# Loads of four batches moved to the head of slabs, and the tile-mode products of a slab joined into one burst, in a fused attention and feed-forward kernel

## Chip, cores, metric

One NeuronCore of a Trainium2 chip. The metric is the device time of one execution in microseconds (us). All runs used here are fast except one execution of the kernel before (480.15 us, left out of all means). A ratio is the mean time of one kernel's fast runs over that of the other's of the same rounds, so it is not quite the ratio of the medians quoted. Kernels are compared only within the same rounds.

## The reference, cut

```python
# q, k, v: 8 batches x 8 heads x 576 rows x 64, float32
q_s = softmax(q, axis=-1)              # along the 64
k_s = softmax(k, axis=2)               # along the 576 rows
kv  = einsum('bhsd,bhse->bhde', k_s, v)      # 64 x 64 a head
x   = einsum('bhsd,bhde->bhse', q_s, kv)     # back to 576 x 64 a head
# x as 4608 tokens x 512
h = x @ w_in                           # 512 -> 2048
g = h * sigmoid(beta * h)
out = g @ w_out                        # 2048 -> 512
```

The feed-forward part is nearly all of TensorE's work: 1152 wide matmuls, at the 0.2158 us that one takes in slab 7 about 249 of the 271.8 us that TensorE is busy (an estimate from the profile before). The attention part of batch b must be ready before the tokens of batch b enter it.

## The kernel before

The tokens are cut into nine slabs of 512: slab b holds the first 512 rows of batch b, slab 8 the 64 remaining rows of all batches. A slab is *pass 1* (64 matmuls of 128x512 with `w_in`, each group of four drained by a SiLU on ScalarE) and *pass 2* (64 with `w_out`). The attention products of the next batches are slipped between the matmuls of pass 2. They use TensorE as four 64x64 tiles at once, four products to a *quad*: 72 key-value products for a batch (eight heads, nine row groups), 8 output products, and every second slab 16 remainder products.

```python
        def kv_quads(b, bks, halves=(0, 2)):       # 36 products for each half
            i = b % 2
            for a in halves:
                for j in range(NG):                # NG = 9
                    for hp, ro, co in quad(a):
                        p = slice(ro, ro + 64)
                        tile_mm(bks[hp % 2], ro, co, VW * (a // 2), D + 1, EK[i][p, hp, j, :],
                                VB[i][p, hp, j, 0:D + 1], j == 0, j == NG - 1,
                                [("ekc", i, hp), ("vb", i, hp, 0), ("vb", i, hp, 1), ("vone", i)])
            for y in range(2 if 2 in halves else 0):
                ...    # VectorE: reciprocal of the sums, KVC = products x reciprocal

        def block(b):
            if b + 1 < B:
                kv_a(b + 1)                        # first half of the next batch
            out_quads(b, (5, 6, 7, 0))             # 8 output products, 4 copies to XT
            if b % 2 and b > 1:
                outr_quads(b, (1, 2))              # 16 remainder products
        ...
            elif t < 7:                            # slab t: what is slipped in, and after how many matmuls
                todo = [(94, lambda: block(t + 1))]
                if t + 2 < B:
                    todo += [(112, lambda: kv_b(t + 2))]   # second half
        ...
            for b in late:                         # pass 2 of slab t, b = t + 2
                exp_q(b)
                ...
                if b + 2 < B and t > 1:
                    load(b + 2)
```

Slots count a slab's matmuls, so slots 65 to 128 are pass 2. The buffers of K (`EK`) and V (`VB`) are double, one for even and one for odd batches.

Every operation is recorded with what it reads and writes; a write waits for all earlier readers of the same buffer. Semaphores are then planned so:

```python
        for op in self.ops:
            op.deps = [d for d in op.deps if not (d.eng == PE and op.eng == PE and d.slot is None)]
            for d in op.deps:
                d.inc = True                       # d will increment its engine's semaphore
        ...
            elif op.inc:                           # numbered in order, one count an engine
                counts[key] = counts.get(key, 0) + 1
                op.count = (key, counts[key])
        ...                                        # a waiter then waits only for the highest count
```

The softmax here doesn't subtract the row's maximum and nothing guards it: scores larger than these inputs give would overflow.

## Time and profile before

| | before |
|---|---|
| time, median (fast runs) | 283.36 us (283.06 to 283.49, 3 runs) |
| span of the profiled run | 280.5 us |
| TensorE busy, granted clock | 97%, 1.00 |
| slabs 1 to 6, start to start | 16.96*, 29.63, 29.35, 29.22, 29.09, 28.41 us |
| slab 7 (wide matmuls alone) | 27.62 us |

*Slab 1 from the start of its pass 2, since its pass 1 is mixed with slab 0. The lengths are differences of the start times of the first pass 1 matmul of each slab, in the view of TensorE in order of time; worked out before rounding, so the last digit can differ by one from the rounded starts; the prediction shows the starts of slabs 2 to 7, and pass 2 of slab 1 starts at 59.38. TensorE, 97% busy, bounds the kernel, so what a slab takes above 27.62 us is what its small products cost.

### The profile page before, as it was taken

Reading aid. Unit: us, or ns where it says so; the run is one execution under the profiler, and the core shown is the slowest. Engines: PE = TensorE matmul, PEld = TensorE weight load, DVE = VectorE, ACT = ScalarE, POOL = GpSimd, SP = SyncE. Lnnn points to the kernel's source line nnn. Section 1 sums busy time; section 2 is a strip of 40 time slices with the busy share of each in tenths; the row PEclk is TensorE's granted clock in tenths of the full one; section 3 lists DMA queues with packets and bytes.
Section 4 is the critical chain, followed back from the end, with each engine's and each line's share of the span. In section 5 each row is a group of like instructions: output and inputs, shape, how many; then the busy total and the mean of one; then the engine's idle time right before and its main releaser. Section 6 shows DMA issues by size and latency. Waiting matters only on the chain.

```text
span 280.5 us, 4478 instructions
## 1 busy us (share of the span) xinstructions
PE 271.8 (97%) x1836; PEld 132.9 (47%) x1870; DVE 104.6 (37%) x211; ACT 169.0 (60%) x242; POOL 36.7 (13%) x56
## 2 busy tenths in 40 slices
PE   7899999999999999999999999999999999999995
PEld 3545454445445544545454444444444444444443
DVE  4754786217490058003740363035704100110012
ACT  5768687989477735794479537871751176017500
POOL 6630041116104030300050000000000000000000
PEclk9999999999999999999999999999999999999999
DMA  7999999999999999509990034001700020011022
GB/s 246 373 390 402 388 382 305 377 332 249 252 371 214 353 301 408 101 7 306 347 108 4 0 128 98 0 4 64 180 1 0 40 112 0 0 74 78 0 72 78
DMA packets 42044, 50.10 MB, mean 179 GB/s; under 512 B 20900, under 2 KB 29348, under 8 KB 40872
## 3 DMA queue, kind: packets, MB, share of 16 engines
q1 hardware_dynamic: 41072, 48.77, 57.1%
q10 hardware_dynamic: 952, 1.06, 1.1%
q8 instruction: 14, 0.23, 0.3%
q14 instruction: 6, 0.05, 0.1%
HBM read 36.71 MB, written 9.44 MB: 165 GB/s over the span
## 4 chain that ended last, share of the span: by engine, by line
PE 84%; DMA 8%; SPq 3%; DVE 2%; issue 1%
PE PS L390 84%; DMA O2S<-in_moe_w_in_dram 4%; DMA O2S<-in_moe_w_out_dram 4%; SPq L645 1%; SPq L261 1%; DVE QS L356 1%; DVE WOUT L638 1%; SPq L251 0%; PE PS L388 0%; DVE WIN L649 0%; DVE KVC L527 0%; DVE RC L525 0%; DVE QI L357 0%; DVE O2S L799 0%
## 5 line engine op out<-in xcount | busy, mean ns | idle before, releaser
L723 ACT ACTIVATE GT<-PS,BETA 128x512 bf16<-128x512 f32 x144 | 96.8, 689 | 72.9 <-PE PS L390 72.9
L390 PE MATMUL PS<-WOUT,GT 128*128 128x512 bf16 (+2 forms) x571 | 126.4, 373 | 2.2 <-issue 1.4
L390 PE MATMUL PS<-XT,WIN 128*128 128x512 bf16 x564 | 125.8, 379 | 0.6
L390 PEld LDWEIGHTS PS<-XT,WIN 128*128 128x128 bf16 x576 | 60.6, 106 | 63.1 <-ACT GT L723 0.4
L390 PEld LDWEIGHTS PS<-WOUT,GT 128*128 128x128 bf16 x592 | 56.0, 98 | 64.2 <-issue 1.0
L778 DVE COPY O2S<-PS 128x512 f32<-128x512 f32 x33 | 22.6, 685 | 109.6 <-PE PS L390 109.5
L375 POOL CAST VB<-VF 128x576 bf16<-128x576 f32 x29 | 21.5, 741 | 77.9 <-DMA VF<-in_v_dram 43.8
L356 DVE TENSOR_REDUCE QS<-EQ 128x8 f32<-128x512 bf16 (+1 forms) x22 | 20.0, 910 | 14.9 <-ACT EQ L320 14.9
L320 ACT ACTIVATE EQ<-QF 128x512 bf16<-128x512 f32 x32 | 17.8, 616 | 2.4 <-DMA QF<-in_q_dram 2.2
L339 ACT ACTIVATE EK<-KF 128x1152 bf16<-128x1152 f32 (+1 forms) x16 | 15.9, 1035 | 1.8 <-DMA KF<-in_k_dram 1.6
L358 DVE TENSOR_TENSOR EQ<-EQ,QI 128x1024 bf16<-128x1024 bf16 (+1 forms) x14 | 15.8, 1128 | 0.5
L540 DVE CAST XT<-PS 128x512 bf16<-128x512 f32 x12 | 7.7, 685 | 17.3 <-PE PS L390 17.3
L540 ACT CAST XT<-PS 128x512 bf16<-128x512 f32 x12 | 6.4, 589 | 11.2 <-PE PS L390 11.2
L358 POOL TENSOR_TENSOR EQ<-EQ,QI 128x512 bf16<-128x512 bf16 x8 | 8.3, 1042 | 27.4 <-DVE QI L357 27.1
L390 PEld LDWEIGHTS PS<-VB,EK 64*64 64x64 bf16 x504 | 6.5, 107 | 5.9 <-issue 4.9
L390 PE MATMUL PS<-VB,EK 64*64 64x65 bf16 x504 | 8.3, 193 | 0.1
L525 DVE RECIPROCAL RC<-PS 128x2 f32<-128x2 f32 x12 | 2.0, 164 | 13.5 <-PE PS L390 13.5
L390 PE MATMUL PS<-XT 128*128 128x512 f32 x6 | 5.5, 1088 | 1.5 <-DVE XT L221 1.5
L723 ACT ACT_TABLE_LOAD x5 | 6.4, 1283 | 0.1
L332 ACT ACTIVATE EKD<-KF 64x576 bf16<-64x576 f32 (+1 forms) x6 | 5.0, 841 | 1.0 <-DMA KF<-in_k_dram 0.9
L357 DVE RECIPROCAL QI<-QS 128x8 f32<-128x8 f32 (+1 forms) x22 | 5.0, 225 | 0.8
L339 ACT ACT_TABLE_LOAD x4 | 5.1, 1283 | 0.1
(62 smaller groups left out, 86.3 us busy)
## 6 DMA issues: line engine op xcount, KB each, us to landing
out_dram<-O2S SPq DMA_DIRECT2D x8, 1024.0 KB, 5.6
QF<-in_q_dram SPq DMA_DIRECT2D x30, 256.0 KB, 6.3
KF<-in_k_dram SPq DMA_DIRECT2D x6, 1152.0 KB, 8.0
VF<-in_v_dram SPq DMA_DIRECT2D x6, 1152.0 KB, 10.9
KF<-in_k_dram SPq DMA_DIRECT2D x8, 288.0 KB, 8.4
VF<-in_v_dram SPq DMA_DIRECT2D x8, 288.0 KB, 8.7
WST<-in_moe_w_in_dram SPq DMA_DIRECT2D x8, 256.0 KB, 8.0
O2S<-in_moe_w_in_dram SPq DMA_DIRECT2D x4, 512.0 KB, 11.7
```

What stands on the lines that cost most here:

```text
L261: add(engs[c % len(engs)], lambda e, a=a, o=o: e.dma_start(o, a), w=[(name, i, hp) for hp in range(c * n, c * n + n)], slot=f"{name}{i}_{c}")
L320: add(ACTE, lambda e, o=o, a=a: e.activation(o, a, ACT.Exp), r=[("qf", i, hp)] if b < 2 else [("qf", i, hp, x) for x in ((2, 3) if hp % 2 ...
L332: add(ACTE, lambda e: e.activation(o, a, ACT.Exp), r=[("kf", i, h) for h in hps], w=[("ek", i, h, e_) for h in hps])
L339: add(ACTE, lambda e: e.activation(o, a, ACT.Exp), r=[("kf", i, h) for h in range(hp, hp + n)], w=[("ekc", i, h) for h in range(hp, hp + n)])
L356: add(DVE, lambda e: e.tensor_reduce(s_, a, AX.X, ALU.add), r=ks, w=[("qs", i, hp0)])
L357: add(DVE, lambda e: e.reciprocal(v_, s_), r=[("qs", i, hp0)], w=[("qi", i, hp0)])
L358: add(eng, lambda e: e.tensor_tensor(a, a, vb, ALU.mult), r=ks + [("qi", i, hp0)], w=ks)
L375: add(eng, lambda e: (e.copy if eng == ACTE else e.tensor_copy)(o, a), r=[("vf", i, hp), ("vone", i)], w=[("vb", i, hp, h) for h in ((0, 1 ...
L390: add(PE, lambda e: e.matmul(o, l, r_, start=start, stop=stop, tile_position=tp), r=r, w=w, bank=[bk])
L540: add(eng, lambda e, eng=eng, bk=bk, hp=hp: (e.copy if eng == ACTE else e.tensor_copy)(XT[i][:, hp, :], PS[bk][:, :]), r=[("ps", bk)], w=[ ...
L723: add(ACTE, lambda e: e.activation(GT[:, f, :], PS[bk][:, :], ACT.Silu, scale=BETA[:, f:f + 1]), r=[("ps", bk), "beta"], w=[("gt", f)], ba ...
L778: add(eng, lambda e: (e.copy if eng == ACTE else e.tensor_copy)(O2S[t % 2][:, u, :], PS[bk][:, :]), r=[("ps", bk)], w=[("o2", t % 2, u)], ...
```

## The change

Two intents: no loads beside the small products of pass 2, and one entry into tile mode a slab for two. The diff, cut (the functions were only split into products and copies, so that all products of a burst come before all copies):

```diff
         def block(b):
+            rem = b % 2 and b > 1
             if b + 1 < B:
-                kv_a(b + 1)
-            out_quads(b, (5, 6, 7, 0))
-            if b % 2 and b > 1:
-                outr_quads(b, (1, 2))
+                kv_prods(b + 1, (1, 2), (0, 2))
+            out_prods(b, (5, 6, 7, 0))
+            if rem:
+                outr_prods(b, (1, 2))
+            out_evac(b, (5, 6, 7, 0))
+            if rem:
+                outr_evac(b, (1, 2))
+            if b + 1 < B:
+                kv_evac(b + 1, (1, 2))
 ...
-                         (116, lambda: block(2)), (124, lambda: kv_b(3))]
+                         (116, lambda: block(2))]
             elif t < 7:
-                todo = [(94, lambda: block(t + 1))]
-                if t + 2 < B:
-                    todo += [(112, lambda: kv_b(t + 2))]
+                todo = [(104, lambda: block(t + 1))]
 ...
             if 2 <= t < 7:
+                if t < 5:
+                    load(t + 2 if t == 2 else t + 3)
 ...
-                if b + 2 < B and t > 1:
-                    load(b + 2)
 ...
-                    load(4)
```

## The prediction

> **What bounds the kernel now.** I read the page's busy shares first, then the chain that ended last, then TensorE alone in order of time, and last the few microseconds around the tile-mode products in a stage with loads and in one without.

> ```profile
> PE 271.8 (97%) x1836; PEld 132.9 (47%) x1870; DVE 104.6 (37%) x211; ACT 169.0 (60%) x242; POOL 36.7 (13%) x56
> ...
> PEclk9999999999999999999999999999999999999999
> ...
> PE 84%; DMA 8%; SPq 3%; DVE 2%; issue 1%
> ```

> TensorE is busy 97% of the span at its full clock, and 84% of the chain is TensorE; the 8% of DMA and most of the rest lie in the first 38 us, which the change does not touch. So only what shortens TensorE's own stream can help. TensorE in order of time, from slab 4 on (start, us, engine, group):

> ```profile
> 135.32 13.98 PE L390 MATMUL PS<-XT,WIN 128*128 128x512 bf16 x63
> ...
> 164.54 13.98 PE L390 MATMUL PS<-XT,WIN 128*128 128x512 bf16 x63
> ...
> 193.63 13.98 PE L390 MATMUL PS<-XT,WIN 128*128 128x512 bf16 x63
> ...
> 222.05 13.98 PE L390 MATMUL PS<-XT,WIN 128*128 128x512 bf16 x63
> 235.86 13.98 PE L390 MATMUL PS<-WOUT,GT 128*128 128x512 bf16 x63
> 249.67 13.98 PE L390 MATMUL PS<-XT,WIN 128*128 128x512 bf16 x62
> ```

> Slab 7 holds nothing but 128 wide matmuls: 249.67 - 222.05 = 27.62 us, or 0.2158 us each. What any other slab takes above 27.62 is the price of its tile-mode products. Slab 2 starts at 76.34, slab 3 at 105.97, slab 4 at 135.32 (the same view, earlier). Their excesses are: slab 2 2.01, slab 3 1.73, slab 4 1.60, slab 5 1.47, slab 6 0.79. Slabs 2 and 4 have equal work (key-value products of one batch, the output products and the remainder products), and so have slabs 3 and 5 (no remainder). Yet 2 costs 0.41 more than 4, and 3 costs 0.26 more than 5. The timeline shows where, first for slab 2 and then for slab 4:

> ```profile
> 97.09 0.34 PEld L390 LDWEIGHTS PS<-QT,KVC 64*64 64x64 bf16 x8
> 97.37 0.62 PEld L390 LDWEIGHTS PS<-QTR,KVC 64*64 64x64 bf16 x16
> 98.25 3.83 PE L390 MATMUL PS<-WOUT,GT 128*128 128x512 bf16 x17 [0.16 <-issue]
> 102.01 0.44 PEld L390 LDWEIGHTS PS<-VB,EK 64*64 64x64 bf16 x36 [0.42 <-issue]
> 102.73 3.40 PE L390 MATMUL PS<-WOUT,GT 128*128 128x512 bf16 x15 [0.16 <-issue]
> ```

> ```profile
> 155.99 0.15 PEld L390 LDWEIGHTS PS<-QT,KVC 64*64 64x64 bf16 x8
> 156.24 0.39 PEld L390 LDWEIGHTS PS<-QTR,KVC 64*64 64x64 bf16 x16
> 156.90 3.83 PE L390 MATMUL PS<-WOUT,GT 128*128 128x512 bf16 x17 [0.16 <-issue]
> 160.66 0.37 PEld L390 LDWEIGHTS PS<-VB,EK 64*64 64x64 bf16 x36 [0.42 <-issue]
> 161.30 3.40 PE L390 MATMUL PS<-WOUT,GT 128*128 128x512 bf16 x15 [0.16 <-issue]
> ```

> Two things show. Each entry into tile mode stops the weight loads for 0.42 us, and each exit leaves 0.16 us of TensorE idle, though nothing is being waited for. And all small products run slower in slab 2. The sums by stretch give the one difference I can name (the last two columns are the DMA share and GB/s):

> ```profile
> 97.00:103.00 6.00, 5.68 (x105) 3.37 (x94) 2.55 (x5) 2.36 (x3) 1.34 (x3) 1.00 1.14 300
> 126.80:132.50 5.70, 5.38 (x67) 2.70 (x66) 1.89 (x3) 2.36 (x3) 0.00 (x0) 1.00 0.95 306
> 155.50:161.50 6.00, 5.68 (x116) 2.99 (x117) 2.83 (x7) 2.48 (x4) 0.00 (x0) 1.00 0.00 0
> ```

> Loads were running in slabs 2 and 3, and none in slab 4. The granted clock was 1.00 in all three.

> [...] 0.44 against 0.37 us for 36 weight loads. [...] I count this cost, without knowing its mechanism.

> **The change part by part.** No work is added or removed. TensorE's order changes only from slab 1 on.

> *One burst for two.* In slabs 2 to 5 the 36 later key-value products leave slot 112 and the first burst moves from slot 94 to one joint burst at slot 104; in slab 1 slots 116 and 124 become 116. The separate burst's price, without loads: from 156.90 to 161.30 stand 18 wide matmuls (94 to 112), 4.40 - 18 x 0.2158 = 0.52 us. With loads: 98.25 to 102.73, 0.60 us. What 36 such products cost inside a burst: slab 5's first burst is 1.47 - 0.52 = 0.95 (36 key-value and 8 output products); the remainder is (1.60 - 0.52) - 0.95 = 0.13; slab 6's burst has 8 output and 16 remainder products for 0.79, so 8 outputs cost 0.66 and 36 key-value products 0.95 - 0.66 = 0.29. Saved per merge: 0.52 - 0.29 = 0.23 without loads; with loads I take 0.21 (0.60 less an estimated 0.39). All of it is on the path.

> *No loads beside the burst.* Slab 1: batch 4's loads leave it (issued from 69.88, burst at 72.12; batch 3's last remainder load lands at about 72.04), so its burst should run at the quiet rate: 0.26, as between slabs 3 and 5. Slab 3: batch 7's loads (from 124.74) move to slab 4's head, and batch 6's (issued 96.86) to slab 3's head, issued at about 107 to 111 and landed by some 122, before the burst near 127.5: 0.26. Slabs 4 and 5 had no loads beside their bursts already: 0. Slab 2: batch 5's loads still follow batch 4's loads and three transposes on the one SyncE queue, so I expect them issued from about 88 on and in flight until about 103, around the burst at about 98.5. I count 0 there; if it were quiet it would be 0.41.

> The sum: slab 1 0.21 + 0.26, slab 2 0.21, slab 3 0.23 + 0.26, slabs 4 and 5 0.23 each: 1.63 us. Vector and scalar work is the same in number; only its order moves. After the joint burst VectorE has two XT copies (1.29), the remainder copies (0.74) and the key-value pair (about 0.9): 2.9 us, and 24 wide matmuls (5.2 us) remain before pass 1 wants XT and banks 0 to 2. In slab 1 only 12 remain (2.6 us), but pass 1 wants first XT (about 2.0 us after the products) and bank 1 only four matmuls later; it fits.

> **The rivals.** *A late load stalls slab 2.* Batch 4's loads now start behind the store of slab 1, at about 78, and pass 2 of the same slab uses them from 91. The page has K landing a median 8.0 us and V 10.9 us after their issue, so K lands near 89.5 and V near 92.5; ScalarE wants K at 92.35, after its table load; the casts of V take 2.9 us and end near 95.5, the burst is at 98.5. Slack 3 us; a miss would cost 1 to 2 us, 283 to 284. For it: a 1 MB store stands ahead, and loads alone needed 14.4 us from first issue (69.88) to the first cast of V (84.24), with a store in the midst. Against it: even 14.4 us after 78 gives 92.4.

> *Late transposes stall slab 2 or 4.* The transposes of the next batch now stand behind a whole load. In slab 4 that load has eight small remainder pieces and took SyncE 10.4 us to issue before (124.74 to 135.14). From 136 that ends at about 146.5; two transposes and the remainder's take 4 to 5 us more, and land some 3 us later, at about 154; the burst is near 157. Slack about 3 us; again about 1 us if missed, 282.8.

> *The transfers do not slow the products at all* and slabs 4 and 5 were quicker for another reason (place in the program). Then only the merging pays: 1.1 us, 282.4. Against it: the slow and fast rates split exactly by whether the DMA share was near 1 or 0, in four slabs. *Slab 2 quiet too*: 281.4.

> **The range and the chances.** 283.49 - 1.63 = 281.86; the quick runs of before were 283.49 and 283.06, so I say 281.8. The rivals span 281.4 to about 283, with 0.3 us between runs: 281.0 to 282.8. Two per cent is 5.7 us, more than all excesses in slabs 1 to 5 that the change touches could return; a gain that large is out of reach, a loss that large needs stalls in several slabs.

> **What would show it.** Right: slabs 4 and 5 shorter by 0.23 us each (29.0 and 28.86), slab 3 near 28.86 with its weight loads at the 0.15 us rate, one 0.42 us stop per slab, slab 2 near 29.4 and still at the slow rate. Wrong: TensorE idle in front of the burst with a releaser such as the V casts, the K exponentials or a transposed QT, at about 98 or 157 us; a pass 1 that now waits for XT; or a slab 3 burst that is slow although no load runs.

The wide matmuls took the same time with loads and without, 13.81 us from start to start for pass 1 of slab 2, at a DMA share of 1.11, and for that of slab 7, at 0.18. The 0.44 against 0.37 us is the contrast to it: 36 small weight loads in slab 2 and in slab 4.

## The result

The changed kernel is slower by 0.4%, a small loss but clear of the noise: 284.57 us median (284.09 to 285.02, 4 runs) against 283.36; ratio 1.0044, 95% interval 1.0022 to 1.0067. Executions over 1.5% slower than the fastest of the same kernel are left out of the means. The profiled spans are 282.3 against 280.5 us. The forecast of 281.8 (281.0 to 282.8) missed, in sign too.

The same slab lengths, from the same view, say where:

| slab | before | after | difference | predicted |
|---|---|---|---|---|
| 1 (pass 2) | 16.96 | 17.59 | +0.63 | -0.47 |
| 2 | 29.63 | 30.27 | +0.64 | -0.21 |
| 3 | 29.35 | 29.99 | +0.64 | -0.49 |
| 4 | 29.22 | 29.05 | -0.17 | -0.23 |
| 5 | 29.09 | 28.93 | -0.17 | -0.23 |
| 6, 7 | 28.41, 27.62 | 28.41, 27.62 | 0 | 0 |

Their sum is +1.57 us; another 0.2 us of the 1.8 us between the profiled ends of TensorE's work lies before slab 1, where the two kernels' TensorE streams are the same. So slabs 4 and 5 did about what was predicted, and slabs 1 to 3 the opposite. The row of slab 1 is the least sure: the mean times differ by 1.26 us, not 1.8, and the later experiments list spans of 280.4 to 281.9 us for the kernel before, so its profiled run (280.5) was a quick one. Slabs 2 to 7 repeat to 0.01 us in every profile of equal bursts; slab 1 doesn't (see the first experiment). TensorE in order of time, in slab 3 and then in slab 4 of the changed kernel (start, us, engine, group, count):

```profile
121.26 8.80 PE L390 MATMUL PS<-WOUT,GT 128*128 128x512 bf16 x40
129.99 1.79 PE L390 MATMUL PS<-VB,EK 64*64 64x65 bf16 x72
131.62 0.69 PE L390 MATMUL PS<-QT,KVC 64*64 64x512 bf16 x8
132.24 5.35 PE L390 MATMUL PS<-WOUT,GT 128*128 128x512 bf16 x24
...
159.97 0.83 PE L390 MATMUL PS<-VB,EK 64*64 64x65 bf16 x72
160.62 0.62 PE L390 MATMUL PS<-QT,KVC 64*64 64x512 bf16 x8
161.05 0.31 PE L390 MATMUL PS<-QTR,KVC 64*64 64x64 bf16 x16
161.29 5.35 PE L390 MATMUL PS<-WOUT,GT 128*128 128x512 bf16 x24
```

The same 72 products take 1.79 us in slab 3 and 0.83 in slab 4. No wait is named before either. And the loads are not it: the sums by stretch over the bursts of slabs 2, 3 and 4 (the last two columns again the DMA share and GB/s).

```profile
99.70:102.25 2.55, 2.55 (x97) 2.49 (x96) 0.00 (x0) 0.00 (x0) 0.00 (x0) 1.00 0.98 342
129.98:132.22 2.24, 2.24 (x81) 1.95 (x80) 0.00 (x0) 0.00 (x0) 0.00 (x0) 1.00 0.03 7
159.96:161.28 1.32, 1.32 (x97) 1.11 (x96) 0.21 (x1) 0.14 (x1) 0.00 (x0) 1.00 0.00 0
```

Slab 3's burst now has no loads beside it, as predicted, and is as slow as slab 2's, which has. The start times of the single products show the form of the loss. Differences from one start to the next, in ns, worked out from the trace of the changed kernel:

```
slab 3:  3 4 3 42 4 3 3 26 4 3 3 23 3 4 4 21 4 0 4 21 4 6 3 22 3 4 3 22 3 5 3 22 19 | 34 34 34 34 35 34 34 34 34 34 35 ... 34 34 34
slab 4:  3 3 4 42 3 4 3 26 3 4 3 22 4 3 3 23 3 0 4 22 3 5 4 22 4 3 3 23 3 3 4 23 3   | 0 3 63 4 3 3 19 27 3 4 3 25 1 2 4 23 ... 21 4 3
```

Up to the 33rd product the two are alike: four start together, and a quad takes about 33 ns, 8 ns a product. From there on slab 4 goes on so, while in slab 3 each product comes 34 ns after the last.

What is different in slabs 1 to 3? Not the work, the data's shape or the waits: the built programs have four waits in each 72 products in all five slabs. But counting semaphore increments in the built program, I find 72 of 72 key-value products incrementing in slabs 1, 2 and 3, none of 72 in slab 4 and 2 of 72 in slab 5. The difference comes from the helper shown above. The exponentials of batch b + 2 overwrite the `EK` that batch b's products read, so each of these products is a dependence and gets an increment. Batches 6 and 7, whose products run in slabs 4 and 5, have no successor. The helper lets waiters wait for the highest count alone, but it never takes back the increments that nobody then needs: TensorE makes 1473 increments, of which 255 are needed.

### The profile page after: what moved, and what is told of

Read it like the earlier page. It is cut to its first block, busy times and chain, and to the rows that moved or that the text cites. A ratio compares the mean times of both kernels' runs of the same rounds, so it can differ in the third digit from the quotient of the medians.

```text
span 282.3 us, 4505 instructions
## 1 busy us (share of the span) xinstructions
PE 276.4 (98%) x1870; PEld 135.4 (48%) x1870; DVE 105.0 (37%) x211; ACT 169.3 (60%) x242; POOL 35.6 (13%) x56
## 3 DMA queue, kind: packets, MB, share of 16 engines
q10 hardware_dynamic: 952, 1.06, 1.1%
## 4 chain that ended last, share of the span: by engine, by line
PE 80%; DMA 12%; SPq 4%; ACT 2%; DVE 1%; issue 0%; ACTq 0%
PE PS L390 80%; DMA QRF<-in_q_dram 4%; DMA WST<-in_moe_w_out_dram 4%; DMA WST<-in_moe_w_in_dram 4%; SPq L261 2%; ACT GT L738 1%; SPq L660 1%; DVE WOUT L653 1%; ACT L913 0%; SPq L251 0%; SPq L270 0%; ACT EQR L345 0%; DVE WIN L664 0%; DVE O2S L814 0%; ACT DUMMY L913 0%
## 5 line engine op out<-in xcount | busy, mean ns | idle before, releaser
L390 PE MATMUL PS<-WOUT,GT 128*128 128x512 bf16 (+2 forms) x592 | 128.4, 373 | 0.0
L390 PE MATMUL PS<-XT,WIN 128*128 128x512 bf16 x576 | 126.7, 379 | 0.1
L390 PEld LDWEIGHTS PS<-XT,WIN 128*128 128x128 bf16 x576 | 60.5, 106 | 63.4 <-ACT GT L738 0.6
L390 PEld LDWEIGHTS PS<-WOUT,GT 128*128 128x128 bf16 x592 | 56.4, 98 | 65.3 <-issue 1.0
L375 POOL CAST VB<-VF 128x576 bf16<-128x576 f32 x29 | 20.4, 702 | 91.1 <-DMA VF<-in_v_dram 89.8
L390 PEld LDWEIGHTS PS<-VB,EK 64*64 64x64 bf16 x504 | 8.6, 106 | 3.8 <-issue 2.6
L390 PE MATMUL PS<-VB,EK 64*64 64x65 bf16 x504 | 10.0, 192 | 0.2
L390 PE MATMUL PS<-XT 128*128 128x512 f32 x6 | 5.5, 1088 | 1.5 <-DVE XT L221 1.5
L345 ACT ACTIVATE EQR<-QRF 128x512 bf16<-128x512 f32 x4 | 2.5, 622 | 3.4 <-DMA QRF<-in_q_dram 3.4
```

The costliest lines, as they stand in the source:

```text
L375: add(eng, lambda e: (e.copy if eng == ACTE else e.tensor_copy)(o, a), r=[("vf", i, hp), ("vone", i)], w=[("vb", i, hp, h) for h in ((0, 1 ...
L390: add(PE, lambda e: e.matmul(o, l, r_, start=start, stop=stop, tile_position=tp), r=r, w=w, bank=[bk])
```

## The experiments

Six edits tell B from the prediction's theory A (loads beside the products slow them) and take B apart; one looks for a better kernel; one pair repeats a reading. All gave correct results. Slab lengths below are from the profiled run of each, in the same view.

### Loads moved alone

```diff
+                if t < 5:
+                    load(t + 2 if t == 2 else t + 3)      # and the two loads in pass 2 removed
-                todo = [(94, lambda: block(t + 1))]
+                todo = [(104, lambda: block(t + 1))]
-                    todo += [(112, lambda: kv_b(t + 2))]
+                    todo += [(118, lambda: kv_b(t + 2))]
```

> The kernel before with the loads moved as in the change, but two bursts a slab as before (first at slot 104, second at slot 118, so that the later transposes are in time). Theory A (mine on record: loads running beside the small products slow them): slabs 1 and 3 become 0.26 us shorter each, total 0.5 us under before, ratio 0.998. Theory B (each key-value product that increments a semaphore costs about 34 ns once the first 33 of a burst are through; loads do nothing): slab 2 stays at 29.63, slab 3 at 29.35 us, intervals of 34 ns stay after the 33rd product of each first burst, ratio 1.000 within 0.001.

Measured: 283.14 us median of 5, ratio 1.0005 (0.9988 to 1.0021). Slab 2 29.63, slab 3 29.35. TensorE in order of time in slab 3, then the sums of that stretch:

```profile
129.33 0.56 PE L390 MATMUL PS<-VB,EK 64*64 64x65 bf16 x36
129.74 0.69 PE L390 MATMUL PS<-QT,KVC 64*64 64x512 bf16 x8
...
129.30:130.90 1.60, 1.44 (x47) 1.02 (x48) 0.05 (x1) 0.00 (x0) 0.00 (x0) 1.00 0.00 0
```

DMA share 0.00, and the 36 products still take the slow 0.56 us. Theory A falls; moving the loads is worth nothing by itself.

Slab 1 met neither theory: its pass 2 took 17.70 us, 0.74 more than in the profile before, since TensorE waited there for a transposed QT:

```profile
73.14 0.90 PE L390 MATMUL PS<-QT,KVC 64*64 64x512 bf16 x8 [0.38 <-DMA QT<-EQ]
```

These transposes are issued from about 65.5 us on in both kernels (65.50 and 65.59), before the moved load, so the move doesn't explain the wait. When they land differs: at 72.15 and 72.59 us in the profile before, at 73.54 and 74.03 in that of the changed kernel. And slab 1 differs from profile to profile even of one kernel (17.02 and 17.37 us in two profiles of the third experiment's first kernel).

### Bursts joined alone

```diff
-                if t < 5:
-                    load(t + 2 if t == 2 else t + 3)
+                if b + 2 < B and t > 1:                   # loads back where they were
+                    load(b + 2)
```

> The changed kernel with the loads put back where they were. Theory A in its last form (the joint burst is bad because loads run beside it in slabs 1 and 2): slab 3 would now be no better than 29.99, since batch 7's loads run beside it again, and the total above that of after. Theory B: the same as after, ratio to before 1.004, slabs 2 and 3 at 30.27 and 29.99, slabs 4 and 5 at 29.05 and 28.93.

Measured: 284.98 us median of 6, ratio 1.007 (1.005 to 1.009). Slabs 2 to 5: 30.26, 29.99, 29.05, 28.93, as after to 0.01. So the joining alone makes the slab differences. The ratio missed the expected 1.004: it is 0.003 above the changed kernel's, though the intervals overlap. The spans average 282.7 us for both kernels, so the excess lies outside the core's span, where no trace shows it.

### Increments only where one is waited for

In the planning helper, on the changed kernel and on the one before:

```diff
             op.deps = [d for d in op.deps if not (d.eng == PE and op.eng == PE and d.slot is None)]
+            last = max((d.pos for d in op.deps if d.eng == PE), default=-1)
+            op.deps = [d for d in op.deps if d.eng != PE or d.pos == last]
```

> The changed kernel in which a matmul increments the semaphore only where somebody waits for that very matmul (each waiter keeps the last of the TensorE instructions it depends on[...]); increments on TensorE fall from 1473 to 255, products with 72 of 72 to 4 of 72. Theory B: all bursts run at the rate of slabs 4 and 5; slab 2 from 30.27 to about 29.05 or a little less, slab 3 from 29.99 to about 28.93, slab 1 about 1.1 less; total 3.3 to 3.6 us under after, about 281.0, ratio to before 0.992. Theory A: slab 2, with batch 5's loads still running beside its burst, stays above 30.

> The kernel before with the same sparing of increments; its loads stay beside the bursts of slabs 2 and 3. Theory B: slab 2 from 29.63 to 29.22, slab 3 from 29.35 to 29.09, slab 1 about 0.3 less: total about 1.0 us under before, ratio 0.9965. Theory A: slabs 2 and 3 stay 0.41 and 0.26 us longer than slabs 4 and 5.

Measured: the changed kernel 281.10 us median of 6, ratio 0.9933 (0.9916 to 0.995), slabs 2 to 5 29.05, 28.93, 29.05, 28.93. The kernel before 282.00 us median of 5, ratio 0.9963 (0.9947 to 0.9978), slabs 2 to 5 29.22, 29.10, 29.21, 29.10. All results were correct, so waiting for the last of TensorE's instructions was enough. The burst of slab 2 in the changed kernel with spared increments, which took 1.79 us before:

```profile
98.92 0.83 PE L392 MATMUL PS<-VB,EK 64*64 64x65 bf16 x72
```

Equal work now takes equal time in slabs 2 to 5. In the kernel before the loads still ran beside slab 2's burst; the sums by stretch of its first burst in slab 2 and in slab 4:

```profile
97.27:98.13 0.86, 0.86 (x61) 0.66 (x60) 0.12 (x1) 0.08 (x1) 0.00 (x0) 1.00 0.92 297
155.58:156.44 0.86, 0.86 (x61) 0.65 (x60) 0.12 (x1) 0.07 (x1) 0.00 (x0) 1.00 0.00 0
```

The same instructions in the same 0.86 us, at a DMA share of 0.92 and of 0. That settles theory A. And between these two kernels joining does what the prediction wanted of it: 0.17 us a slab in slabs 2 to 5. Slab 1 missed what was expected, again with waits of TensorE for a transposed QT (0.19 and 0.33 us): 17.02 us in the changed kernel (0.57 less, not 1.1) and 17.37 in the kernel before (0.42 more, not 0.3 less).

### Increments added where there were none

```diff
+                        if b > 5:                         # in the loop of kv_prods
+                            P.ops[-1].inc = True
```

> The changed kernel with the suspected cost added where it was missing: every key-value product of batches 6 and 7 (bursts of slabs 4 and 5, which have no loads beside them) also increments the semaphore, though nobody waits for it: 144 products, of which 2 incremented it already. If the increments are the cost: slab 4 goes from 29.05 to the 30.27 of slab 2 and slab 5 from 28.93 to the 29.99 of slab 3, each with intervals of 34 ns from the 33rd product on; total 2.3 us over after, ratio to before about 1.0125. If the place in the program or the data of the early batches made slabs 1 to 3 slow: no change from after, 1.004.

Measured: 286.65 us median of 4, ratio 1.0128 (1.0113 to 1.0143). Slab 4 30.27, slab 5 29.99. Slab 4 in order of time:

```profile
159.95 1.79 PE L390 MATMUL PS<-VB,EK 64*64 64x65 bf16 x72
161.59 0.69 PE L390 MATMUL PS<-QT,KVC 64*64 64x512 bf16 x8
162.02 0.54 PE L390 MATMUL PS<-QTR,KVC 64*64 64x64 bf16 x16
```

1.79 us for 0.83: 142 increments that nobody waits for move the slow form, to the hundredth, into slabs that had been quick. The place in the program and the data are ruled out.

### Increments taken from the key-value products alone

```diff
+                        P.ops[-1].quiet = j < NG - 1      # in kv_prods
 ...
-            op.deps = [d for d in op.deps if not (d.eng == PE ...)]
+            op.deps = [d for d in op.deps if not d.quiet and not (d.eng == PE ...)]
```

> The changed kernel with increments taken only from the key-value products of the tiled bursts (8 of 72 keep theirs); all other matmuls keep theirs. If it is these products alone: slabs 2 and 3 at 29.05 and 28.93 as with the increments spared everywhere, total near 281.3, ratio to before 0.993. If the increments of the wide matmuls before the burst matter too (a backlog of theirs): between that and after.

Measured: 282.18 us median of 4, ratio 0.997 (0.995 to 0.999). Slabs 2 and 3 are 29.11 and 28.98, within 0.06 of all spared (8 of 72 still increment), so it is these products. But the time missed the expected 281.3. It was run again beside the kernel with all spared:

> The kernel with increments spared on the tiled key-value products alone once more, beside the one with all spared, because its ratio (0.997) missed the expected 0.993 although its slabs 2 to 5 were as short as expected and its profile lost 0.8 us before 29 us. If that was start-up scatter of the few runs: ratio 0.993 to 0.995 now, as the other. If the increments of the other matmuls cost something by themselves: again near 0.997, some 0.3 per cent above the other.

> The kernel with all spare increments of TensorE taken away, once more as the yardstick on the same chip: ratio 0.993 within 0.002.

Measured: 281.62 us, ratio 0.9955 (0.994 to 0.997), and 281.21 us, ratio 0.9931 (0.9913 to 0.995). The intervals overlap, so a difference in time between the two is not shown; the spans lean to one, 279.8 and 279.6 us on the mean for the two tries against 279.1 with all spared. Both profiles of the first start slab 0's pass 2 0.7 us later (29.35 and 29.28 us, against 28.56 and 28.64). Whether the increments of slab 0's small products have to do with that stays open: the kernels before and after have them too, and start it at 28.53. In both profiles slab 1 was then short, 16.43 us, with no wait for QT.

### Half the increments

```diff
+                        P.ops[-1].quiet = ro != co and (j < NG - 1)   # two of each quad
```

> The changed kernel with increments on every other pair of key-value products (40 of 72). If a product with an increment is handed out only every 34 ns or so[...]: the knee stays at about the 33rd product, the 39 after it take about half of 34 ns each on the mean (0.7 us, against 1.33 with all and 0.32 with none), slab 2 near 29.65. If instead finished increments pile up and the pile holds about 25: no knee within 72 products, slab 2 near 29.1.

Measured: 283.20 us median of 4, ratio 1.0008 (0.9986 to 1.0029). Slab 2 29.62, slab 3 29.49. The 72 products in slab 2:

```profile
98.97 1.35 PE L391 MATMUL PS<-VB,EK 64*64 64x65 bf16 x72
```

1.35 us, between 0.83 and 1.79. The differences of start times, in ns as above:

```
slab 2:  3 3 4 42 4 3 3 26 ... 3 4 3 23 19 | 8 8 86 3 4 3 23 35 8 8 34 35 8 8 34 35 8 8 34 35 8 8 34 ...
```

The knee is still at the 33rd product, and from the 41st on two products of each quad come after 34 to 35 ns and two after 8. So the cost goes with the number of increments, not with a mode of the burst, and a pile of about 25 increments as the limit (no knee within 72) is ruled out. The 25 was an estimate: at 34 ns each, about 8 of the 33 would be through in the 0.283 us that 33 starts take. Why the first 33 are quick is not shown; no run tests it by itself. One trace bears on it: in slab 1 of the changed kernel the 39th product waits for a cast of V and starts 230 ns after the 38th, and the eight products behind it start within 85 ns; then it is 34 ns each again.

### A better kernel

All compute engines' spare increments taken away, and slab 1's burst at slot 119:

```diff
-            op.deps = [...]                               # keep of each engine the last dependence
+            op.deps = [d for d in op.deps if d.slot is not None or last[d.eng] is d]
-                         (116, lambda: block(2))]
+                         (119, lambda: block(2))]
```

> The fastest version so far, with the same sparing of increments on all compute engines (each waiter keeps the last instruction of each engine that it depends on) and the burst of slab 1 at slot 119 instead of 116, because the run with spared increments waited there some 0.5 us for a transposed QT. Expected: slab 1 0.4 us shorter, the other engines' increments worth nothing as TensorE bounds: 280.7, ratio to before 0.992. If the nine wide matmuls left after the burst are too few, TensorE waits for XT or bank 1 at the start of slab 2 and the gain is lost.

Measured: 281.10 us median of 6, ratio 0.993 (0.9915 to 0.9946). Slab 1's pass 2 fell to 16.38 us, from 17.02 and 17.37 in the two profiles with the burst at 116; two edits were made at once, and slab 1 varies, so this isn't put down to the slot. The total, expected at 280.7, can't be told from the kernel with TensorE's increments alone (0.9933 and 0.9931). Both beat before and after.

## Why the prediction was wrong, point by point

- *TensorE bounds, and slabs above 27.62 us show the cost of small products*: right, and it is what made the miss readable.
- *No loads beside the burst: 0.26 us in slabs 1 and 3*: **the step that failed.** It rested on two pairs of slabs (2 against 4, 3 against 5) that differed in the DMA share. They also differed in increments, 72 against 2, which no view of the profile shows. With spare increments gone, loads cost nothing (0.86 and 0.86 us, at DMA shares of 0.92 and 0). The slow rate's form was in the trace before, too: in slab 3's first burst the last three steps, after the 33rd product, are 20, 34 and 34 ns; in slab 4's they are 4, 0 and 3. I had only looked at the sums of 36.
- *One burst for two: 0.21 to 0.23 us in each of slabs 1 to 5*: right in kind in slabs 4 and 5 and with spare increments gone, but 0.17, not 0.23: joined, 36 more products took 0.83 - 0.48 = 0.35 us, not the 0.29 counted. In slabs 1 to 3 a term is missing. The mean step after the 33rd is (1.600 - 0.283) / 39 = 34 ns, against 8, for 39 products: about 1.0 us, where the two short bursts and what followed them had lost 0.26 (slab 3 less slab 5 before). Slab 3 less slab 5 after is 1.06, close to that 1.0. The rest is bookkeeping: 1.06 - 0.26 - 0.17 = 0.63 is the measured loss a slab.
- *The rivals of late loads and late transposes*: neither came true. The casts of V in slab 2 ended at 96.84, the burst began at 99.72. Transposes stood behind the loads (the second of slab 2 was issued by 93.8 only), but no burst in slabs 2 to 5 waited for one. Batch 5's loads were issued from 95.1, not 88, behind them.
- *Each exit leaves 0.16 us of TensorE idle*: a misreading. The trace before lacks records: 1836 matmuls for 1870 weight loads, the first wide matmul after a burst among the missing (17 shown, 18 in the program). The changed kernel's trace has 1870 of both and names no idle of its matmuls there. No sum rested on the 0.16. That changing the mode costs something stands: with spare increments gone, one entry and exit less saved 0.17 us a slab.
- *Slab 2 keeps its loads beside the burst*: right (share 0.98), and of no account.

## What to carry to other kernels

Count the semaphore increments in a burst of small matmuls before joining or moving it; a wide matmul of 216 ns hid one here (in the changed kernel pass 1 took 13.81 us from start to start in slab 3, where all 64 matmuls increment, and in slab 7, where 16 do), a tile product of 8 ns did not: 34 - 8 = 26 ns more for each after the 33rd. So a short burst hides what a long one pays: 36 products took 0.56 us against 0.48, 72 took 1.79 against 0.83. Let the last matmul of a run do the signalling for all of it, as the runs with spared increments did with correct results. And when two stretches differ in time, list all that differs between them, also what the profile does not print, and look at single start times before a cause is named from a sum.
